# Token mixing with centred w1 columns on the split raw x, two plain queries, and DVE, POOL and loads in program order

## The chip, the cores and the metric

One core of one Trainium2 chip runs the whole program. The metric is the device time of one execution in microseconds (us). The kernel before was run three times: 1012.42, 1010.75 and 1012.12 us, so its median is 1012.12 us. The engines are PE (TensorE, matrix products), ACT (ScalarE), DVE (VectorE), POOL (GpSimd) and SP (which here only issues DMAs).

## What is computed

One input x of 2048 tokens by 448 channels goes through an attention (16 heads of 28, one shared key and value) and through a token-mixing MLP, and a gate mixes the two. Everything is float32.

```python
x = A_x
g = _sigmoid((x * gate_w).sum(-1, keepdims=True))
a = _A_ref(x, A_wq, A_wk, A_wv, A_wo)          # softmax(q k / sqrt(28)) v, then @ wo
...
h = _gelu(_layernorm(x, axis=-1) @ w1)         # 448 -> 448
...
hs = concatenate([g0, g1, g2, g3]) @ w2        # four channel groups shifted by +1, -1, +2, -2 tokens
x1 = x + hs
h2 = _gelu(_layernorm(x1, axis=-1) @ w3) @ w4  # 448 -> 1792 -> 448
...
return g * a + (1 - g) * (x1 + h2)
```

The layernorm has no weights: (x - m) / sqrt(v + eps). Because the mean over channels is linear, (x - m) @ w1 equals x @ (w1 minus the mean of each of its columns), and the division by the deviation is one factor for each token.

## The kernel before

**Arithmetic.** A float32 product is made of fp32r products of a rounded high part and a low part: `proj` (L110 to L116) issues 11 matmuls of 512 columns for a contraction over 448 channels. `proj32` (L118 to L120) is the plain float32 form, 4 matmuls. High parts are casts by ACT, low parts are subtractions by DVE (`split_w`, `split_x`, `split_a`).

**Stages.** Tokens are worked in four blocks of 512. Stage one makes, for each block b, four query tiles (`stage_q(4b)` to `stage_q(4b+3)`, which also carry keys, values and the gate; ACT copies each from PSUM and stores it to a DRAM scratch `qd`), the layernorm of x, `stage_w1(b)` (four tiles of 112 channels, each of 11 matmuls, then two Gelu passes on ACT and a subtraction on POOL) and `stage_w2(b)` (four token tiles of 12 matmuls, each added to x1 by DVE at L360). Stage two is the MLP: in each block 14 steps f, each with `w3_part` (11 matmuls) and `w4_part` for step f-2 (12 matmuls). Stage three is attention. The products of stages one and two go through two PSUM banks (`mm_tile`, tag "mm", two buffers): a product may start when the product two before it has been read out.

**The first layernorm.** `layernorm_stats` takes mean and variance on DVE and the power -0.5 on POOL; `layernorm_norm` makes the normalised rows on DVE and POOL; `layernorm_tile` transposes them on PE (L152, four transposes for each of 16 token tiles) into the "tp" banks, and `split_a` splits them again (ACT L106, DVE L107 and L108). The queries do not need it: they take the transposed x that is loaded as `xT` and split by `split_x`.

**What sets the order.** PE runs in program order throughout. In stage one a block `stage_one` puts DVE and POOL in program order too, up to the middle of the last `stage_w2`; in attention a block `attention` does so for DVE. Everywhere else, and for ACT always, a scheduler orders the instructions from its own estimates. An engine waits at the head of its queue, so what stands behind a waiting instruction waits with it. SP issues nearly all loads; `xraw` has three buffers (tag "raw", shared with `wqraw`), the raw w3 and w4 pieces have one each (`raw3`, `raw4`), so the next piece can be loaded when the last one has been split.

**Late small work.** The gate (`gg`, `gi`, L563 to L566) and the weighing of x1 by 1 - g (L671, 16 tiles on POOL) stand at the start of stage three. The first query's preparation (L535 to L544) stands in block 0 of the MLP, its maxima (`fills`) from block 1 on.

Of the kernel before, what the change touches and what calls it, by code (L numbers as in the profile page):

```python
# [9 lines left out]
F32 = mybir.dt.float32  # L10
# [30 lines left out]
def gated_mix_kernel(  # L41
# [17 lines left out]
    ctx.enter_context(tc.manual_schedule(engines={mybir.EngineType.PE}))  # L59
# [62 lines left out]
    def layernorm_stats(pool, b):  # L122
        pairs = (1, 3) if pool.name == "s1" else (3,)
        mv = pool.tile([P, 4, 2], F32, tag="mv", bufs=2, name=f"mv_{pool.name}_{b}")
        rs = pool.tile([P, 4], F32, tag="rs", bufs=2, name=f"rs_{pool.name}_{b}")
        for t in range(4):
            st = pool.tile([P, 6], F32, tag="st", bufs=4, name=f"st_{pool.name}_{b}_{t}")
            nc.vector.bn_stats(st, x1[:, 4 * b + t, :])
            nc.vector.bn_aggr(mv[:, t, :], st)
            if t in pairs:  # L130
                w = slice(t - pairs[0], t + 1)
                nc.gpsimd.tensor_tensor(rs[:, w], mv[:, w, 1], epst[:, w], ALU.add)
                nc.gpsimd.tensor_tensor(rs[:, w], rs[:, w], powt[:, w], ALU.pow)
        return mv, rs
# [3 lines left out]
    def layernorm_norm(pool, b, t, mv, rs):  # L138
        xt = x1[:, 4 * b + t, :]
        xn = pool.tile([P, 512], F32, tag="xn", bufs=3 if pool.name == "s1" else 4, name=f"xn_{pool.name}_{b}_{t}")  # L140
        nc.vector.tensor_scalar(xn[:, 0:D], xt, mv[:, t, 0:1], rs[:, t:t + 1],
                                op0=ALU.subtract, op1=ALU.mult)
        nc.gpsimd.tensor_copy(xn[:, D:512], xn[:, 384:D])
        xn_of[t] = xn
# [79 lines left out]
    with tc.tile_pool(name="s1b", bufs=1) as s1b, \  # L224
# [26 lines left out]
        for g in range(1, 4):  # L251
            nc.sync.dma_start(wqraw[:, 0:3, g * P:(g + 1) * P], wq[:, 0:3, g * P:(g + 1) * P])
        nc.sync.dma_start(wqdup[64:128], wq[64:128, 3, :])
        w1h = s1.tile([P, 4, D], F32R, name="w1h")
# [15 lines left out]
        def stage_q(u):  # L270
            b, g = divmod(u, NG)
            ps = mm_tile(f"q_{u}")
            w = slice(g * P, (g + 1) * P)
            if u < 4:
                proj32(ps, lambda c: wqraw[:, c, w], wqraw[:, 3, w], xraw[0])
            else:
                proj(ps, wqh[:, :, w], wql[:, :, w], *xact[b])
            qf = s1.tile([P, 512], F32, tag="qf", bufs=3, name=f"qf_{u}")
            nc.scalar.copy(qf, ps)
            nc.scalar.dma_start(qd[g, :, 512 * b:512 * b + 512], qf)  # L280
# [30 lines left out]
        def ln1_begin(b):  # L311
            ah = s1.tile([P, 4, 512], F32R, tag="ah", bufs=3, name=f"ah1_{b}")
            al = s1.tile([P, 3, 512], F32R, tag="al", bufs=3, name=f"al1_{b}")
            acts[b] = (ah, al, *layernorm_stats(s1, b))

        def ln1_tile(b, t):
            ah, al, mv, rs = acts[b]
            layernorm_tile(s1, tp_tile, b, t, mv, rs, ah, al)

        def ln1_norm(b, t):  # L320
            layernorm_norm(s1, b, t, *acts[b][2:4])
# [6 lines left out]
        def stage_w1(b, after):  # L328
            hh[b] = s1b.tile([P, 4, 516], F32R, tag="hh", bufs=2, name=f"hh_{b}")
            hl[b] = s1b.tile([P, 4, 516], F32R, tag="hl", bufs=2, name=f"hl_{b}")  # L330
            for m in range(4):
                ps = mm_tile(f"h_{b}_{m}")
                w = slice(m * C, (m + 1) * C)
                proj(ps[0:C, :], w1h[:, :, w], w1l[:, :, w], *acts[b][0:2])
                for job in after.get(m, ()):
                    job()
                hf = s1.tile([P, 512], F32, tag="hf", bufs=2, name=f"hf_{b}_{m}")
                nc.scalar.activation(hh[b][0:C, m, 2:514], ps[0:C, :], AF.Gelu_apprx_tanh)
# [26 lines left out]
        load_x1(0)  # L365
# [3 lines left out]
        load_x1(1)  # L369
# [6 lines left out]
        def ln_jobs(b):  # L376
            def step(t):
                ln1_tile(b, t)
                if t < 3:
                    ln1_norm(b, t + 1)  # L380
            return {m: (lambda t=m - 1: step(t),) for m in (1, 2, 3)}

        stage_one = ExitStack()
        stage_one.enter_context(tc.manual_schedule(
            engines={mybir.EngineType.PE, mybir.EngineType.DVE, mybir.EngineType.Pool}))
        stage_q(0)
        split_w(wqraw, wqh, wql, slice(0, 256), wqdup)
        stage_q(1)
        split_w(wqraw, wqh, wql, slice(256, 512), wqdup)
        stage_q(2)  # L390
        split_x(1, ((0, 2), (2, 4)))
        stage_q(3)
        ln1_begin(0)
        stage_q(4)
        ln1_norm(0, 0)
        ln1_norm(0, 1)
        ln1_norm(0, 2)
        stage_q(5)
        split_w(w1raw, w1h, w1l)
        ln1_tile(0, 0)  # L400
        ln1_norm(0, 3)
        ln1_tile(0, 1)
        stage_q(6)
        ln1_tile(0, 2)
        ln1_tile(0, 3)
        stage_q(7)
        ln1_begin(1)
        split_x(2, ((0, 2), (2, 4)))
        ln1_norm(1, 0)
        stage_w1(0, ln_jobs(1))  # L410
        stage_kv(0)
        stage_q(8)
        split_w2()
        ln1_tile(1, 3)
        stage_q(9)
        ln1_begin(2)
        ln1_norm(2, 0)
        stage_w1(1, ln_jobs(2))
        stage_kv(1)
        stage_w2(0)  # L420
        split_k(0)
        stage_q(10)
        ln1_tile(2, 3)
        stage_q(11)
        split_x(3, ((0, 2), (2, 4)))
        ln1_begin(3)
        ln1_norm(3, 0)
        stage_w1(2, ln_jobs(3))
        stage_kv(2)
        stage_w2(1)  # L430
        split_k(1)
        stage_q(12)
        ln1_tile(3, 3)
        mv0, rs0 = layernorm_stats(s1b, 0)
# [3 lines left out]
        stage_w1(3, {})  # L438
# [11 lines left out]

        def load_w34(i, pool):
            load_w3(i, pool)
            load_w4(i, pool)

        def load_w3(i, pool):
            w3h.append(pool.tile([P, 4, 2 * P], F32R, name=f"w3h_{i}"))
            w3l.append(pool.tile([P, 4, 2 * P], F32R, name=f"w3l_{i}"))
            raw = s2a.tile([P, 4, 256], F32, tag="raw3", bufs=1, name=f"w3raw_{i}")
            nc.sync.dma_start(raw, w3[:, :, i * 256:i * 256 + 256])
            split_w(raw, w3h[i], w3l[i])  # L460

        def load_w4(i, pool):
            w4h.append(pool.tile([P, 2, D], F32R, name=f"w4h_{i}"))
            w4l.append(pool.tile([P, 2, D], F32R, name=f"w4l_{i}"))
            raw = s2a.tile([P, 2, D], F32, tag="raw4", bufs=1, name=f"w4raw_{i}")
            nc.sync.dma_start(raw, w4[i * 256:i * 256 + 256, :].rearrange("(c p) n -> p c n", p=P))
            nc.scalar.copy(w4h[i], raw)
            nc.vector.tensor_tensor(w4l[i], raw, f32(w4h[i]), ALU.subtract)
# [12 lines left out]
        ln_begin(0, (mv0, rs0))  # L481
        for t in range(4):
            layernorm_norm(s2a, 0, t, *acts[0][2:4])
# [3 lines left out]
        stage_w2(NB - 1, lambda t: load_w3(0, s2a) if t == 0 else load_w4(0, s2a) if t == 1 else None)  # L487
        stage_one.close()
        for i in range(1, 3):
            load_w34(i, s2a)  # L490

    with tc.tile_pool(name="s2", bufs=1, reuse_waits="tile") as s2, \
            tc.tile_pool(name="ps2", bufs=1, space=PSUM, reuse_waits="tile") as ps2:
        fills = [lambda t=t: max_part(0, t, max_tile) for t in range(4)]
# [27 lines left out]
        for b in range(NB):  # L522
            acc = [ps2.tile([P, 512], F32, tag="acc", bufs=4, name=f"acc_{b}_{t}") for t in range(4)]
            gs = {}
            for f in range(NF):
                if f == NF - 3 and b + 1 < NB:
                    ln_begin(b + 1)
                if f == NF - 1 and b + 1 < NB:
# [3 lines left out]
                if b == 0 and f % 2 and f < 8:  # L532
                    load_w34((f + 5) // 2, s2a if f == 1 else s2)
                if b == 0 and f == 9:
# [4 lines left out]
                    q_load(0, s2.tile([P, 512], F32, tag="gf", bufs=2, name="qr_0"))  # L539
                    q_split(0, qh0, s2.tile([P, 512], F32R, tag="gl", bufs=3, name="ql_0"))  # L540
                    q_rows(0)
                if f >= 2:
                    for t in range(4):
                        w4_part(f - 2, t, gs[f - 2], acc)  # L544
                        if b > 0 and t % 2 == 0 and f < NF - 1:
# [15 lines left out]
    with tc.tile_pool(name="s3", bufs=1, reuse_waits="tile") as s3, \  # L561
            tc.tile_pool(name="ps3", bufs=1, space=PSUM, reuse_waits="tile") as ps3:
        nc.gpsimd.tensor_tensor(gg, invE, gz, ALU.pow)  # L563
        nc.vector.tensor_scalar(gg, gg, 1.0, None, op0=ALU.add)
        nc.vector.reciprocal(gg, gg)
        nc.vector.tensor_scalar(gi, gg, -1.0, 1.0, op0=ALU.mult, op1=ALU.add)  # L566

# [102 lines left out]
        for n in range(NT):  # L670
            nc.gpsimd.tensor_scalar(x1[:, n, :], x1[:, n, :], gi[:, n:n + 1], None, op0=ALU.mult)  # L671
# [31 lines left out]
        attention = ExitStack()  # L703
        attention.enter_context(tc.manual_schedule(engines={mybir.EngineType.PE, mybir.EngineType.DVE}))
# [38 lines left out]
        attention.close()  # L743
# [125 lines left out]
```

## Time and profile before

| | |
|---|---|
| median of three runs | 1012.12 us |
| the profiled execution's own time | 1012.79 us |
| its span, first to last instruction | 1011.2 us |
| mean granted TensorE clock | 0.996 |
| stage one (to the first w3 matmul) | 0 to 148.5 us |
| MLP (to the first attention matmul) | 148.5 to 432 us |
| attention and the tail | 432 to 1011.2 us |
| ACT / DVE / POOL busy over the span | 660.0 / 291.5 / 120.9 us |

The profile is one execution. A row of the timeline gives the start in us, the busy time in us, the engine, the line, the operation, and what was written from what; in brackets stands the idle time of that engine just before, with what ended it. Rows of matmuls overlap, because matmuls are pipelined: the pace of PE is read from start to start. A row of the waits gives who waited for whom: us in total, number of times, longest.

### The profile page before, as it was taken

What the parts mean: (1) busy time and instruction counts of PE and PEld (TensorE: products, weight loads), DVE (VectorE), ACT (ScalarE), POOL (GpSimd) and SP (SyncE); (2) the same over time, 40 slices, a digit from 0 to 9 for tenths busy, and PEclk for the clock granted to TensorE, in tenths of its full rate; (3) what the DMA queues carried; (4) which work ended last, traced back from release to release, by engine and by line L of the source; (5) the groups of instructions that cost most, each with busy time, mean ns of one, the idle gap of its engine ahead of it and who ended that gap; (6) DMA issues with size and microseconds to landing.
All of it is one profiled execution on the core that took longest, in us unless ns stands there. A gap on an engine that the chain in (4) does not pass through costs nothing.

```text
span 1011.2 us, 13843 instructions
## 1 busy us (share of the span) xinstructions
PE 994.1 (98%) x5336; PEld 647.7 (64%) x5336; DVE 291.5 (29%) x618; ACT 660.0 (65%) x1290; POOL 120.9 (12%) x176
## 2 busy tenths in 40 slices
PE   9999989999999999999999999999999999999996
PEld 4787878888888888854554554555455455545553
DVE  5645375342141131131222222222221222222113
ACT  4532325322232232289999989989998998999894
POOL 3333350020020020050000000000000000000000
PEclk9999999999999999999999999999999999999999
DMA  8600215200000000021011101101120110121001
GB/s 286 247 22 24 91 42 157 76 1 1 1 1 1 0 1 0 19 66 39 12 28 38 38 29 49 38 11 30 38 75 2 39 38 11 48 57 29 2 2 40
DMA packets 34085, 43.68 MB, mean 43 GB/s; under 512 B 9004, under 2 KB 22108, under 8 KB 34012
## 3 DMA queue, kind: packets, MB, share of 16 engines
q1 hardware_dynamic: 31228, 38.20, 13.1%
q10 hardware_dynamic: 2784, 4.52, 1.2%
q8 instruction: 44, 0.72, 0.3%
q14 instruction: 29, 0.24, 0.1%
HBM read 23.15 MB, written 7.86 MB: 31 GB/s over the span
## 4 chain that ended last, share of the span: by engine, by line
PE 92%; DVE 3%; POOL 1%; DMA 1%; ACT 1%; issue 0%; SPq 0%; POOLq 0%; ACTq 0%
PE bank L718 26%; PE pv L694 23%; PE acc L518 4%; PE acc L520 4%; PE acc L519 4%; PE g L112 4%; PE g L114 4%; PE g L113 4%; PE q L120 2%; PE bank L652 2%; PE bank L187 1%; PE bank L656 1%; PE bank L654 1%; PE g L115 1%; PE g L116 1%; PE h L113 1%
## 5 line engine op out<-in xcount | busy, mean ns | idle before, releaser
L720 ACT ACTIVATE p<-bank 128x512 f32<-128x512 f32 x1024 | 515.1, 629 | 47.9 <-PE bank L718 45.4
L718 PE MATMUL bank<-qs,kS 98*128 98x512 f32 x1024 | 316.3, 411 | 0.5 <-DVE x L556 0.5
L718 PEld LDWEIGHTS bank<-qs,kS 98*128 98x128 f32 x1024 | 183.2, 189 | 147.6 <-issue 106.5
L694 PE MATMUL pv<-p,vext 128*32 128x512 f32 x2048 | 246.5, 598 | 0.0
L508 ACT ACTIVATE gh<-g 128x512 fp32r<-128x512 f32 x56 | 33.5, 599 | 156.5 <-PE g L116 156.4
L694 PEld LDWEIGHTS pv<-p,vext 128*32 128x32 f32 x2048 | 54.8, 109 | 114.6 <-issue 108.9
L188 DVE TENSOR_REDUCE mr<-bank 128x4 f32<-128x512 f32 x60 | 41.6, 693 | 168.3 <-PE bank L187 168.3
L510 DVE TENSOR_TENSOR gl<-gf,gh 128x512 fp32r<-128x512 f32 x56 | 38.6, 691 | 158.6 <-ACT gf L509 154.2
L661 DVE SCALAR_TENSOR_TENSOR ot<-bank,gg,ot 128x448 f32<-128x448 f32 x48 | 32.8, 684 | 174.7 <-PE bank L656 89.0
L518 PE MATMUL acc<-w4h,gh 128*128 128x448 f32 x224 | 82.1, 367 | 0.0
L520 PE MATMUL acc<-w4h,gl 128*128 128x448 f32 x224 | 81.5, 364 | 0.0
L519 PE MATMUL acc<-w4l,gh 128*128 128x448 f32 x224 | 81.3, 363 | 0.0
L639 POOL CAST onh<-on 128x512 fp32r<-128x512 f32 x15 | 9.2, 612 | 501.4 <-DVE on L636 501.4
L112 PE MATMUL g<-ah,w3h 128*128 128x512 f32 x168 | 66.0, 393 | 0.9 <-ACT gf L509 0.9
L114 PE MATMUL g<-ah,w3l 128*128 128x512 f32 x168 | 65.6, 391 | 0.0
L113 PE MATMUL g<-al,w3h 128*128 128x512 f32 x168 | 65.6, 391 | 0.0
L519 PEld LDWEIGHTS acc<-w4l,gh 128*128 128x128 f32 x224 | 42.1, 188 | 4.3
L518 PEld LDWEIGHTS acc<-w4h,gh 128*128 128x128 f32 x224 | 42.1, 188 | 4.2
L520 PEld LDWEIGHTS acc<-w4h,gl 128*128 128x128 f32 x224 | 42.1, 188 | 3.2
L671 POOL TENSOR_SCALAR x<-x,gi 128x448 f32<-128x448 f32 x16 | 23.1, 1458 | 130.0 <-DVE x L556 130.0
L114 PEld LDWEIGHTS g<-ah,w3l 128*128 128x128 f32 x168 | 31.5, 188 | 6.8
L112 PEld LDWEIGHTS g<-ah,w3h 128*128 128x128 f32 x168 | 31.6, 188 | 6.7 <-ACT gf L509 1.3
(186 smaller groups left out, 1022.3 us busy)
## 6 DMA issues: line engine op xcount, KB each, us to landing
qs<-qh SPq DMA_DIRECT2D x32, 224.0 KB
qd<-qf ACTq DMA_DIRECT2D x16, 256.0 KB
x<-in_x_dram SPq DMA_DIRECT2D x4, 896.0 KB
w3raw<-in_w_dram SPq DMA_DIRECT2D x7, 512.0 KB
qr<-qd SPq DMA_DIRECT2D x16, 224.0 KB
qs<-ql SPq DMA_DIRECT2D x16, 224.0 KB
out_dram<-ot SPq DMA_DIRECT2D x16, 224.0 KB
w4raw<-in_w_dram SPq DMA_DIRECT2D x7, 448.0 KB
```

The costliest lines, as they stand in the source:

```text
L112: nc.tensor.matmul(ps, wh[:, c, :], ah[:, c, :], start=(c == 0), stop=False)
L113: nc.tensor.matmul(ps, wh[:, c, :], al[:, c, :], start=False, stop=False)
L114: nc.tensor.matmul(ps, wl[:, c, :], ah[:, c, :], start=False, stop=False)
L188: nc.vector.reduce_max(mx_of[u][:, :, t], ps, axis=AX.X)
L508: nc.scalar.activation(gh, ps, AF.Gelu_apprx_tanh)
L510: nc.vector.tensor_sub(gl, gf, f32(gh))
L518: nc.tensor.matmul(ps, gh[:, tok], w4h[i][:, k, :], start=(f == 0), stop=False)
L519: nc.tensor.matmul(ps, gh[:, tok], w4l[i][:, k, :], start=False, stop=False)
L520: nc.tensor.matmul(ps, gl[:, tok], w4h[i][:, k, :], start=False, stop=(f == NF - 1))
L694: nc.tensor.matmul(pv[32 * j:32 * j + 32, :], vext[:, kt, :], ps[j], start=(kt == 0), stop=(kt == NT - 1), tile_position=(0, 32 * j))
L718: nc.tensor.matmul(ps, kS[0:98, kt * P:(kt + 1) * P], q_of[u][0:98, j, :], start=True, stop=True)
L720: nc.scalar.activation(p, ps, AF.Exp, scale=SCALE)
```

## The change

1. **No normalised x for w1.** `stage_w1` now multiplies the split raw x (`xact[b]`, the same operand as the queries) by w1 whose columns have been centred. POOL sums w1 over its row chunks (`sum_w1`), one plain float32 matmul with a matrix of ones sums over partitions, and DVE subtracts the mean from w1 (`centre_w1`) before w1 is split. The 1/deviation of each token is stored to DRAM, loaded back broadcast over 112 partitions (`ln1`), and DVE multiplies it onto each product; the two Gelu passes then read that from SBUF. The 64 transposes, the normalised rows and their split are gone.
2. **Two plain queries instead of four**; x of block 0 is now split as well.
3. **Order.** DVE, POOL and SP run in program order for the whole kernel, and the program's text is rearranged: loads stand where they are to be issued, `stage_w1(0)` and `stage_w1(1)` follow each other, each w3/w4 piece's load is separated from its split, the normalisation for the next MLP block has its own place at f = 12, the first query's preparation and maxima move one block later, the gate moves to MLP block 1, and twelve of the sixteen weighings of x1 to MLP block 3.

```diff
-    ctx.enter_context(tc.manual_schedule(engines={mybir.EngineType.PE}))
+    ctx.enter_context(tc.manual_schedule(
+        engines={mybir.EngineType.PE, mybir.EngineType.DVE, mybir.EngineType.Pool, mybir.EngineType.SP}))
...
-            if u < 4:
+            if u < 2:
                 proj32(ps, lambda c: wqraw[:, c, w], wqraw[:, 3, w], xraw[0])
...
+        def ln1(b):
+            _, rs = layernorm_stats(s1, b)
+            rd = dram.tile([1, 512], F32, tag="rsd", bufs=2, name=f"rsd_{b}")
+            nc.sync.dma_start(rd.rearrange("o (t p) -> p (o t)", p=P), rs)
+            rb_of[b] = s1.tile([P, 512], F32, tag="rsb", bufs=2, name=f"rsb_{b}")
+            nc.sync.dma_start(rb_of[b][0:C], rd.broadcast_to([C, 512]))
...
+        def sum_w1():
+            nc.gpsimd.tensor_tensor(wsum, w1raw[:, 0, :], w1raw[:, 1, :], ALU.add)
+            nc.gpsimd.tensor_tensor(wsum, wsum, w1raw[:, 2, :], ALU.add)
+            nc.gpsimd.tensor_tensor(wsum[0:64], wsum[0:64], w1raw[0:64, 3, :], ALU.add)
+
+        def centre_w1():
+            ps = misc_tile("wsum_ps")[:, 0:D]
+            nc.tensor.matmul(ps, ones, wsum, start=True, stop=True)
+            for c in range(4):
+                nc.vector.scalar_tensor_tensor(w1raw[:, c, :], ps, -1.0 / D, w1raw[:, c, :],
+                                               op0=ALU.mult, op1=ALU.add)
...
-                proj(ps[0:C, :], w1h[:, :, w], w1l[:, :, w], *acts[b][0:2])
...
-                hf = s1.tile([P, 512], F32, tag="hf", bufs=2, name=f"hf_{b}_{m}")
-                nc.scalar.activation(hh[b][0:C, m, 2:514], ps[0:C, :], AF.Gelu_apprx_tanh)
-                nc.scalar.activation(hf[0:C, :], ps[0:C, :], AF.Gelu_apprx_tanh)
+                proj(ps[0:C, :], w1h[:, :, w], w1l[:, :, w], *xact[b])
+                hf = s1.tile([P, 512], F32, tag="hf", bufs=3, name=f"hf_{b}_{m}")
+                nc.vector.tensor_mul(hf[0:C, :], ps[0:C, :], rb_of[b][0:C, :])
+                nc.scalar.activation(hh[b][0:C, m, 2:514], hf[0:C, :], AF.Gelu_apprx_tanh)
+                nc.scalar.activation(hf[0:C, :], hf[0:C, :], AF.Gelu_apprx_tanh)
...
+        load_x1(0)
+        load_x1(1)
+        stage_q(0)
+        split_x(0, ((0, 2), (2, 4)))
+        split_w(wqraw, wqh, wql, slice(256, 512), wqdup)
+        stage_q(1)
+        stage_q(2)
+        split_w(wqraw, wqh, wql, slice(0, 256), wqdup)
+        split_x(1, ((0, 2), (2, 4)))
+        stage_q(3)
+        sum_w1()
+        ln1(0)
+        load_x(2)
...
+        stage_q(4)
+        centre_w1()
+        stage_q(5)
+        stage_q(6)
+        split_w(w1raw, w1h, w1l)
+        ln1(1)
+        load_x(3)
+        load_x1(3)
         stage_q(7)
...
+        stage_w1(0)
+        split_w2()
         split_x(2, ((0, 2), (2, 4)))
...
+        stage_w1(1)
+        stage_kv(1)
+        ln1(2)
         stage_q(8)
...
+        def weights(t):
+            if t % 2 == 0:
+                split_w3(t // 2)
+            else:
+                split_w4(t // 2)
+                load_w34(t // 2 + 1, s2a)
+
+        stage_w2(NB - 1, weights)
...
+                if b == 1 and f == 0:
+                    nc.gpsimd.tensor_tensor(gg, invE, gz, ALU.pow)
...
+                if b == NB - 1 and f == 4:
+                    weigh_x1(0, 4 * b)
```

More of the change, by code (lines that the diff above doesn't have):

```diff
@@ L129, in layernorm_stats @@
             nc.vector.bn_aggr(mv[:, t, :], st)
[L130 to L133, printed above, removed]
+        nc.gpsimd.tensor_tensor(rs, mv[:, :, 1], epst, ALU.add)
+        nc.gpsimd.tensor_tensor(rs, rs, powt, ALU.pow)
         return mv, rs
@@ L309, in stage_v @@
             nc.vector.tensor_copy(gz.rearrange("p (b t) -> p t b", t=4), vp[:, :, :, DH])
[L311 to L321, printed above, removed]
+        rb_of = {}
+        def ln1(b):
[4 more added lines that the diff above has]
+            nc.sync.dma_start(rb_of[b][0:C], rd.broadcast_to([C, 512]))
+        ones = s1.tile([P, P], F32, name="ones")
+        nc.gpsimd.memset(ones, 1.0)
+        wsum = s1.tile([P, 512], F32, tag="hf", bufs=3, name="wsum")[:, 0:D]
+        def sum_w1():
[8 more added lines that the diff above has]
+                                               op0=ALU.mult, op1=ALU.add)
         def split_w2():
@@ L372, in gated_mix_kernel @@
         load_x1(2)
+        stage_q(4)
[4 more added lines that the diff above has]
+        ln1(1)
         load_x(3)
         load_x1(3)
[L376 to L405, printed above, removed]
         stage_q(7)
-        ln1_begin(1)
+        stage_w1(0)
+        split_w2()
         split_x(2, ((0, 2), (2, 4)))
-        ln1_norm(1, 0)
-        stage_w1(0, ln_jobs(1))
         stage_kv(0)
+        stage_w1(1)
+        stage_kv(1)
+        ln1(2)
         stage_q(8)
-        split_w2()
-        ln1_tile(1, 3)
         stage_q(9)
[L416 to L421, printed above, removed]
         stage_q(10)
-        ln1_tile(2, 3)
         stage_q(11)
         split_x(3, ((0, 2), (2, 4)))
-        ln1_begin(3)
-        ln1_norm(3, 0)
-        stage_w1(2, ln_jobs(3))
+        split_k(0)
         stage_kv(2)
+        ln1(3)
+        stage_w2(0)
+        stage_w1(2)
+        mv0, rs0 = layernorm_stats(s1b, 0)
+        split_k(1)
         stage_w2(1)
-        split_k(1)
         stage_q(12)
-        ln1_tile(3, 3)
-        mv0, rs0 = layernorm_stats(s1b, 0)
         stage_q(13)
@@ L527, in gated_mix_kernel @@
                     ln_begin(b + 1)
+                if f == NF - 2 and b + 1 < NB:
+                    for t in range(4):
+                        layernorm_norm(s2a, b + 1, t, *acts[b + 1][2:4])
                 if f == NF - 1 and b + 1 < NB:
@@ L668, in gated_mix_kernel @@
         nc.gpsimd.tensor_tensor(wol, woraw, f32(woh), ALU.subtract)
-        for n in range(NT):
-            nc.gpsimd.tensor_scalar(x1[:, n, :], x1[:, n, :], gi[:, n:n + 1], None, op0=ALU.mult)
+        weigh_x1(NT - 4, NT)
         jobs = []
```

68 lines of the change are left out of this document (31 added, 37 removed).

## The prediction

> **What bounds the kernel now.** I read the page first: busy shares, then the chain of waits.
>
> ```profile
> span 1011.2 us, 13843 instructions
> PE 994.1 (98%) x5336; PEld 647.7 (64%) x5336; DVE 291.5 (29%) x618; ACT 660.0 (65%) x1290; POOL 120.9 (12%) x176
> ...
> PE 92%; DVE 3%; POOL 1%; DMA 1%; ACT 1%; issue 0%; SPq 0%; POOLq 0%; ACTq 0%
> ```
>
> PE is busy for 98% of the span and makes 92% of the chain that ends last. An edit is therefore worth the PE work that it takes away or adds and the PE waits that it ends or makes; the rest is cover. So next the waits of PE, and the busy times by stretches of 25 us (this row: length, then PE, PEld, DVE, ACT, POOL busy, granted clock, DMA share, GB/s):
>
> ```profile
> PE hs L356 <- DVE x L360: 3.2, 1, 3.2
> ...
> PE g L112 <- ACT gf L509: 0.9, 1, 0.9
> ...
> PE q L120 <- DMA xkv<-in_xT_dram: 0.7, 1, 0.7
> ```
> ```profile
> 125.00:150.00 25.00, 21.82 (x106) 19.18 (x105) 17.80 (x45) 6.13 (x11) 14.99 (x28) 0.93 0.18 56
> ```
>
> PE is busy for only 21.82 of these 25 us, at a granted clock of 0.93. The timelines of PE, POOL and DVE tell how:
>
> ```profile
> 135.87 0.37 PE L358 MATMUL hs<-w2h,hl 112*128 112x448 f32 x1
> 139.41 0.47 PE L356 MATMUL hs<-w2h,hh 112*128 112x448 f32 x1 [3.18 <-DVE x L360]
> ...
> 140.46 0.57 PE L357 MATMUL hs<-w2l,hh 112*128 112x448 f32 x1
> 140.83 0.57 PE L358 MATMUL hs<-w2h,hl 112*128 112x448 f32 x1
> ```
> ```profile
> 133.57 2.91 POOL L563 TENSOR_TENSOR gg<-invE,gz 128x16 f32<-128x16 f32 x1
> ...
> 136.73 1.01 POOL L133 TENSOR_TENSOR rs_s2a<-rs_s2a,powt 128x4 f32<-128x4 f32 x1
> ```
> ```profile
> 137.77 0.94 DVE L141 TENSOR_SCALAR xn_s2a<-x,mv_s2a,rs_s2a 128x448 f32<-128x448 f32 x2 [5.74 <-POOL rs_s2a L133]
> ```
>
> The scheduler put the gate's power (2.91 us) and the second MLP block's layernorm here. POOL does the gate first, DVE stands 5.74 us at the head of its queue for POOL, and the add to x1 that frees PE's bank is behind it. After 3.18 us idle the matmuls run 0.37 us apart instead of 0.20.
>
> **What is removed.** (a) That stall. The gate moves to MLP block 1, the statistics of block 1 to f = 11 of block 0, and in program order nothing stands between the adds but splits of w3 and w4. Gain: 3.3 us from start to start beyond one step, and nine matmuls at 0.37 against 0.20 us, 1.5 us: 4.8 us.
>
> (b) The wait at MLP step 3: between these starts lie 1.29 us where 0.20 is a step, 1.1 us.
>
> ```profile
> 158.18 0.37 PE L520 MATMUL acc<-w4h,gl 128*128 128x448 f32 x1
> 159.47 0.50 PE L112 MATMUL g<-ah,w3h 128*128 128x512 f32 x1 [0.92 <-ACT gf L509]
> ```
>
> The Gelu it waited for stood behind a cast of w4 in ACT's queue; in the changed program it stands ahead of it. What is late next is the w3 piece of step 4, loaded after the split of the piece before, some 2 us earlier in the stage than now. I take the whole 1.1 us.
>
> (c) The transposes for w1, one group of four for each of 16 token tiles:
>
> ```profile
> L152 PE MATMUL tp_s<-ident,xn_s 128*128 128x128 f32 x64 | 9.7, 275 | 1.3 <-DVE xn_s L141 0.9 <-POOL xn_s L143 0.4
> ```
> ```profile
> 42.45 0.60 PE L152 MATMUL tp_s<-ident,xn_s 128*128 128x128 f32 x4
> 42.81 0.47 PE L112 MATMUL h<-ah,w1h 128*112 128x512 f32 x1
> 43.12 0.39 PE L113 MATMUL h<-al,w1h 128*112 128x512 f32 x1
> ```
>
> From start to start a group takes 0.36 us, and the first matmul behind it 0.31 instead of 0.23: 0.44 us, 16 times, 7.0 us. Its waits, 1.3 us, go too.
>
> (d) Two queries become split ones. ACT copies each query out as it ends, so these copies give the pace, plain and then split:
>
> ```profile
> 18.44 0.59 ACT L279 COPY qf<-q 128x512 f32<-128x512 f32 x1 [1.90 <-PE q L120]
> ...
> 21.88 0.59 ACT L279 COPY qf<-q 128x512 f32<-128x512 f32 x1 [0.67 <-PE q L120]
> ...
> 24.39 0.59 ACT L279 COPY qf<-q 128x512 f32<-128x512 f32 x1 [1.34 <-PE q L116]
> ...
> 26.89 0.59 ACT L279 COPY qf<-q 128x512 f32<-128x512 f32 x1 [1.91 <-PE q L116]
> ```
>
> 3.44 against 2.50 us: 1.9 us for two. (e) x's first chunks are now issued ahead of all wq pieces of SP; the 0.7 us wait bounds the gain, and I take 0.4.
>
> Together 4.8 + 1.1 + 7.0 + 1.3 + 1.9 + 0.4 = 16.5 us.
>
> **What is added on PE's path.** (f) The sum of w1's columns is one plain matmul of 448 columns: 3.44 / 4 x 448 / 512 = 0.75 us.
>
> (g) DVE between the first two w1 blocks. In program order the split of w2 and of x block 2 stand behind the fourth multiply of block 0 and ahead of the first multiply of block 1, and that multiply frees the bank that PE wants two products later. The pace of a w1 product is read at two Gelus; a multiply of 512 columns out of PSUM is not in the trace, its nearest row is the maximum over 512 columns of PSUM:
>
> ```profile
> 54.44 0.60 ACT L338 ACTIVATE hh<-h 112x512 fp32r<-112x512 f32 x1 [2.15 <-DMA qd<-qf]
> ...
> 56.97 0.60 ACT L338 ACTIVATE hh<-h 112x512 fp32r<-112x512 f32 x1 [1.45 <-PE h L116]
> ```
> ```profile
> L188 DVE TENSOR_REDUCE mr<-bank 128x4 f32<-128x512 f32 x60 | 41.6, 693 | 168.3 <-PE bank L187 168.3
> ```
> ```profile
> 22.96 1.73 DVE L101 TENSOR_TENSOR w1l<-w1raw,w1h 128x448 fp32r<-128x448 f32 x3
> ...
> 36.26 1.79 DVE L266 TENSOR_TENSOR alk<-xkv,ahk 128x1024 fp32r<-128x1024 f32 x2
> 38.06 0.69 DVE L267 TENSOR_TENSOR ahk<-xkv,ahk 64x512 fp32r<-64x512 f32 x1
> ...
> 48.02 3.17 DVE L326 TENSOR_TENSOR w2l<-w2raw,w2h 112x448 fp32r<-112x448 f32 x4
> ```
>
> From the end of block 0's last product DVE needs 0.69 (multiply), 2.3 to 3.17 (four parts of w2: at w1's rate, or as they ran beside POOL), 1.79 + 0.69 (x) and 0.69 (multiply): 6.2 to 7.0 us. PE is there after two products, 2 x 2.53 = 5.06 us. A wait of 1.1 to 2.0 us; I take 1.6.
>
> (h) The deviation's way through DRAM delays x block 2. On SP the store and the broadcast load of block 0's deviation now stand ahead of the load of x block 2, and in ACT's queue the first cast of that block stands ahead of the copy of query 7, whose bank PE needs for the second w1 product. PE: query 4 started at 21.27, less (d) and (e) 19.0; 4 queries of 2.5, (f) and one product of 2.53 give 32.3 us. The chain against it starts with the statistics, which in the profile run from 18.02:
>
> ```profile
> 18.02 0.63 DVE L128 BATCH_NORM_STATS2 st_s<-x 128x6 f32<-128x448 f32 x1
> ...
> 20.86 0.18 DVE L129 BATCH_NORM_AGGREGATE mv_s<-st_s 128x2 f32<-128x6 f32 x1
> ```
> ```profile
> 964.29 0.62 SPq L615 DMA_DIRECT2D rt<-o  x1
> ```
> ```profile
> 966.21 0.18 DVE L609 SCALAR_TENSOR_TENSOR good<-rt,good 128x16 f32<-128x16 f32 x1 [4.64 <-DMA rt<-o]
> ```
> ```profile
> 144.65 0.61 SPq L459 DMA_DIRECT2D w3raw<-in_w_dram  x1
> ```
> ```profile
> 148.59 0.83 ACT L97 CAST w3h<-w3raw 128x768 fp32r<-128x768 f32 x1 [14.16 <-DMA w3raw<-in_w_dram]
> ```
> ```profile
> 28.50 2.00 ACT L264 CAST ahk<-xkv 128x1024 fp32r<-128x1024 f32 x2
> ```
>
> One more split of x precedes the statistics, but DVE idled before; I take 18.5 to 21.5, then 1.2 on POOL: 22.7. The store moves 512 single floats. The nearest row, 128 pieces of 16 floats, landed 1.92 us after its issue; four times that, 7.7, is the other bound. I take 3, nearer the row, as both move 8 KB or less. Then 0.6 to issue the broadcast. The 1 MB load lies between the 512 KB one (3.94 us to its cast) and twice that, 7.9; I take 6, since the broadcast and the copies of queries share the engines. With the cast (1.0) and the copy (0.6) the bank is free at 33.9: PE waits 1.6 us. Low bounds: 30.7, no wait. High bounds: 40.5, 8.2 us.
>
> (i) On the last w1 block the multiply puts POOL's work 0.69 us later, less a 0.3 us memset moved away, and the first normalised tile of the MLP just met PE before: 0.4 us (0 to 0.9). (j) Queue order elsewhere: 0.5 (0 to 2).
>
> Added: 0.75 + 1.6 + 1.6 + 0.4 + 0.5 = 4.85 us.
>
> **What costs nothing, and its cover.** The other 14 multiplies (0.69) fit in 2.53 us a product, and free the bank sooner than two Gelus did. The centring on DVE (four of 0.69) and the split of w1 behind it have three queries, 7.5 us, and need some 6; without that cover each us late is a us of PE. In the MLP a step is 4.97 us and DVE idles for most of it, which covers maxima, gate and normalisation:
>
> ```profile
> 421.01 0.69 DVE L510 TENSOR_TENSOR gl<-gf,gh 128x512 fp32r<-128x512 f32 x1 [4.27 <-ACT gf L509]
> ```
>
> The weighing, 12 of 1.46 us on POOL, falls where POOL is idle. Attention keeps PE's, ACT's and DVE's order.
>
> **The sum.** 16.5 - 4.85 = 11.65 us. The profiled execution took 1012.79 us, 0.7 above the median of 1012.12; the difference is taken from the median: 1000.5 us.
>
> The Trainium skill, TensorE: Matmul & The Clock Gate, Part 1: The HAM clock gate, says that the clock is halved after an idle window of about 3.4 us. The 3.18 us wait, with a granted clock of 0.93 behind it, roughly agrees. By that rule waits of 1.6 us leave the clock alone and the sum stands; if waits of that length trip it as the long one did, each costs 1.5 us more, and with two of them the sum would be 1003.5 us.
>
> **Rivals.** *The covers hold:* (h), (i) and (j) cost nothing and (g) 1.1: 1012.12 - 16.5 + 1.85 = 997.5 us. For it: every bound's low end; against: the order in ACT's queue.
>
> *x block 2 is late by more:* store 5 and load 7.5 us make (h) 5.1, and a wait that long halves the clock as at 139.41, 1.5: 1005.5. For it: DMA is shared just then.
>
> *The change does not end the stall (a):* DVE now waits in program order for the second w3 piece ahead of the last add; if that reaches PE, 4.8 us stay: 1005.3. Against: no matmul of stage one needs that last add.
>
> *Slower, through the store:* single floats to DRAM are in no row. From a store of about 13 us on (0.4 us for each of the 32 floats that fall to one of 16 engines), the wait (h) with its halved clock eats the whole gain; at 16 us 1015 us. Against: twice the upper bound. The Trainium skill, DMA: Bandwidth & Descriptors, Rules for kernel authors, says that a last dimension without contiguous elements becomes one descriptor for each element, and Specifications, that pieces below 512 B are read, modified and written; it gives no time for them.
>
> **How the numbers follow.** Forecast 1000.5 us, 58%, with its own range 997 to 1004; covers hold 12%; x late 15%; stall stays 7%; slower 8%. The range, 996.5 to 1006.5, takes in the first four but for their tails. 0.2% (2 us) is about what a measurement tells from no change. Faster by more: all of the first two, 13 of 15 and 6 of 7: 89%. Same: 3%. Slower: 8%.
>
> **What would show it.** Right: no transposes before the MLP; query copies 2.5 us apart from the third on; PE without a wait of 3 us at the end of stage one; a wait of PE for DVE of 1 to 2 us at the third product of w1 block 1, and one for ACT near 32 us at the second of block 0; the first w3 matmul near 138 us and attention 578 us long. Wrong: PE waits in the MLP, a clock under 1.0 in stage one, or a store whose broadcast lands after 33 us.

## The result and the profile after

| | before | after |
|---|---|---|
| median, us | 1011.58 (1010.22 to 1014.25, 15 runs) | 1014.84 (1013.10 to 1016.28, 15 runs) |
| ratio to before | | 1.0032, 95% interval 1.0023 to 1.0040 |
| span of the profiled execution, us | 1011.2 | 1012.5 |
| first w3 matmul of the MLP, us | 148.5 | 150.5 |
| first attention matmul, us | 431.96 | 434.18 |

The change made the kernel slower, by 0.2 to 0.4%; 1000.5 us was forecast. The loss lies ahead of the MLP. The page after, then PE's waits (total, times, longest):

```profile
span 1012.5 us, 13677 instructions
...
PE 985.5 (97%) x5280; PEld 642.3 (63%) x5280; DVE 289.0 (29%) x593; ACT 656.5 (65%) x1277; POOL 121.7 (12%) x156
```
```profile
PE h L113 <- ACT qf L277: 12.4, 1, 12.4
PE h L113 <- DVE hf L347: 1.1, 1, 1.1
...
PE m L185 <- DVE mr L186: 0.9, 2, 0.5
...
PE tp_s2a L150 <- POOL xn_s2a L141: 0.7, 1, 0.7
```

PE is busy 8.6 us less than before (994.1 then), though 5.1 us of matmuls ran at half clock: the removed work is gone. The 3.2 us wait of before is gone as well. In its place stands one wait of 12.4 us, at the place of step (h). The stretches of 25 us (columns as in the prediction) and two short ones around the wait:

```profile
25.00:50.00 25.00, 12.62 (x47) 9.49 (x46) 5.97 (x14) 8.16 (x14) 1.22 (x2) 0.74 0.98 149
...
125.00:150.00 25.00, 24.35 (x127) 21.57 (x126) 13.80 (x28) 7.77 (x13) 9.35 (x21) 1.00 0.24 70
```
```profile
36.50:45.40 8.90, 0.00 (x0) 0.00 (x0) 0.69 (x1) 1.54 (x3) 0.00 (x0) 0.51 0.93 235
45.40:50.50 5.10, 5.06 (x12) 3.70 (x13) 0.00 (x0) 3.93 (x7) 0.39 (x1) 0.51 1.17 198
```

The end of the stage, 0.93 in clock before, now runs at 1.00. Between 25 and 50 us PE works half the time. The clock is halved while PE stands, which costs nothing, and for 5.1 us after: 12 matmuls take 5.14 us from start to start where 2.76 is their pace, so about 2.4 us are lost. The wait follows back along three timelines, SP's issues, then ACT, then PE:

```profile
24.09 0.37 SPq L314 DMA_DIRECT2D rsd<-rs_s  x1
34.31 0.34 SPq L316 DMA_DIRECT2D rsb<-rsd  x1
34.88 0.55 SPq L233 DMA_DIRECT2D xkv<-in_xT_dram  x1
...
37.45 0.74 SPq L314 DMA_DIRECT2D rsd<-rs_s  x1
56.32 0.34 SPq L316 DMA_DIRECT2D rsb<-rsd  x1
...
76.31 0.38 SPq L314 DMA_DIRECT2D rsd<-rs_s  x1
85.36 0.30 SPq L316 DMA_DIRECT2D rsb<-rsd  x1
```
```profile
43.85 1.04 ACT L262 CAST ahk<-xkv 128x1024 fp32r<-128x1024 f32 x1 [15.19 <-DMA xkv<-in_xT_dram]
44.81 0.58 ACT L277 COPY qf<-q 128x512 f32<-128x512 f32 x1
```
```profile
32.66 0.40 PE L117 MATMUL h<-ahk,w1l 128*112 128x512 f32 x1
45.44 0.77 PE L113 MATMUL h<-ahk,w1h 128*112 128x512 f32 x1 [12.38 <-ACT qf L277]
```

The broadcast can go out only when the store has landed, and SP issues in order. So the distance between the two issues is the store's time: 10.2 us, 18.9 for the second, which shares the engines with 2.7 MB of loads, and 9.0 for the third. The load of x block 2 goes out 10.8 us after the store; its cast stands ahead of the copy of query 7 in ACT's queue, and that copy frees PE's bank.

What moves meanwhile is seen in the DMA view of 24 to 36 us (40 slices of 0.3 us: busy tenths, then GB/s):

```profile
DMA  9525201000069900090090000090030009969978
GB/s 355 178 61 4 2 0 0 0 0 0 0 232 362 137 0 0 0 27 0 0 14 0 0 0 0 0 20 0 0 7 0 0 0 75 96 68 198 143 184 246
```

Most of the store's time moves nothing at all. The 2.7 MB of loads are not issued yet, because SP stands behind the store; but ACT has handed over two stores of queries (at 26.6 and 28.7 us). Of these 0.2 MB move from 27.3 to 28.2 us, and then next to nothing until 33.9.

### The profile page after: what moved, and what is told of

Same layout as the page of the kernel before. It is cut to its first block, busy times and chain, and to the rows that moved or that the text cites. A ratio compares the mean times of both kernels' runs of the same rounds, so it can differ in the third digit from the quotient of the medians.

```text
span 1012.5 us, 13677 instructions
## 1 busy us (share of the span) xinstructions
PE 985.5 (97%) x5280; PEld 642.3 (63%) x5280; DVE 289.0 (29%) x593; ACT 656.5 (65%) x1277; POOL 121.7 (12%) x156
## 4 chain that ended last, share of the span: by engine, by line
PE 91%; DMA 5%; DVE 2%; ACT 1%; issue 0%; POOL 0%; SPq 0%; ACTq 0%; POOLq 0%
PE bank L722 26%; PE pv L700 23%; PE acc L516 4%; PE acc L518 4%; PE acc L517 4%; PE g L113 4%; PE g L115 4%; PE g L114 4%; DMA rsd<-rs_s 3%; PE bank L659 2%; PE bank L185 1%; PE g L116 1%; PE g L117 1%; PE bank L663 1%; PE bank L661 1%; PE hs L367 1%
## 5 line engine op out<-in xcount | busy, mean ns | idle before, releaser
L114 PEld LDWEIGHTS g<-al,w3h 128*128 128x128 f32 x168 | 31.6, 188 | 5.5
```

The source lines that it names most:

```text
L114: nc.tensor.matmul(ps, wh[:, c, :], al[:, c, :], start=False, stop=False)
```

## Experiments

Each edit is to the changed kernel, unless another is named; `...` in a diff marks lines left out. Waits and spans are those of the profiled execution.

**Size of the pieces.**

```diff
-            nc.sync.dma_start(rd.rearrange("o (t p) -> p (o t)", p=P), rs)
+            k = 2 if b == 2 else 4
+            nc.sync.dma_start(rd.rearrange("o (h p k) -> p (o h) k", p=P, k=k),
+                              rs.rearrange("p (h k) -> p h k", k=k))
```

> The store of the deviations goes out in 128 pieces of 16 bytes (for x block 2 in 256 pieces of 8 bytes) in place of 512 single floats; queues, order and every engine's program stay. The deviations reach other tokens than their own by this. Theory (the number of pieces): store plus its completion fell from 10.2 us to about 2.5 us for the first block, 18.9 to under 6 for the second, about 4.5 for the third (half the pieces of the 9.0) and 2.3 for the fourth (a quarter of the 8.2). The broadcast and the load of x block 2 go out some 7.7 us earlier, ScalarE's cast of that block too, and the 12.4 us wait of TensorE shrinks to about 5 (12.4 - 7.7), with the clock still halved for one or two steps of 3.41 us; span about 1004 (1002 to 1006), ratio to before about 0.993. Rival (a trip through DRAM at this place, whatever its pieces): store still 8 us or more, span 1012. Rival (ScalarE's order alone): the wait only moves, 10 us or more of it stay, span over 1009.

Measured: 1007.76 us, ratio 0.9962 (0.9949 to 0.9976), span 1005.4. SP's queue of this kernel:

```profile
23.88 0.34 SPq L315 DMA_DIRECT2D rsd<-rs_s  x1
26.88 0.34 SPq L318 DMA_DIRECT2D rsb<-rsd  x1
...
32.51 0.35 SPq L315 DMA_DIRECT2D rsd<-rs_s  x1
44.12 0.33 SPq L318 DMA_DIRECT2D rsb<-rsd  x1
...
66.39 0.38 SPq L315 DMA_DIRECT2D rsd<-rs_s  x1
71.00 0.30 SPq L318 DMA_DIRECT2D rsb<-rsd  x1
```

The store takes 3.0 us, the third, of twice as many pieces, 4.6. Only the shape of the pieces differs, and 7 us come back. The second still takes 11.6 us where under 6 was expected: the loads stand ahead of it, and only 7.3 of its 18.9 went with the pieces. PE still waits 5.8 us, since a store of 3.0 us, the broadcast's issue and a load of 9.6 us lie between the deviations and ACT's cast.

**The order on ACT.** `stage_q(7)` to `split_x(3)` are put under a schedule that takes ACT in program order too.

```diff
+        with tc.manual_schedule(engines={mybir.EngineType.PE, mybir.EngineType.DVE, mybir.EngineType.Pool,
+                                         mybir.EngineType.SP, mybir.EngineType.Activation}):
...
```

> ScalarE takes program order too from query 7 to the split of x block 3, so that the copy of query 7 stands ahead of the cast of x block 2; the store stays as it is. Theory (the store with two ways to reach TensorE): query 7 is copied at about 31 us and the second hidden block of the first w1 step runs until 35.5, but the third must wait for the first multiply, which the broadcast releases at 39.9: a wait of about 5 us (40.6 - 35.5) on VectorE's multiply in place of the 12.4 on ScalarE, clock still halved once or twice; span about 1004.5 (1003 to 1007). Rival (ScalarE's order alone): no wait over 1 us is left there, span 997 to 999. Rival (the trip through DRAM is not what holds TensorE): the wait stays at 12 us.

Measured: 1028.39 us, ratio 1.0171 (1.0157 to 1.0185), span 1026.0. PE's waits, then ACT and its DMA issues:

```profile
PE h L113 <- DVE hf L347: 12.7, 2, 6.8
PE hs L366 <- DVE x L370: 9.6, 1, 9.6
```
```profile
77.41 0.59 ACT L277 COPY qf<-q 128x512 f32<-128x512 f32 x1 [1.91 <-PE q L117]
84.25 0.33 ACTq L278 DMA_DIRECT2D qd<-qf  x1
84.62 1.99 ACT L262 CAST ahk<-xkv 128x1024 fp32r<-128x1024 f32 x2 [6.62 <-DMA qd<-qf]
```

At its place the theory holds: the 12.4 us become 5.9. The forecast of the total misses by 21.5 us, because the other stores then come into the open: the second leaves 6.8 us, and during the third, 72.5 to 83.6 us, ACT stands 6.6 us at the issue of a query's store, behind which in program order is the cast that DVE and then PE wait for. So the scheduler's order on ACT alone was not the cause. In the changed kernel the first wait covers the second store: PE comes to the multiply of block 1 so late that the deviations are there. The third wait is of this edit's own making, since there ACT's cast of x block 3 stands behind the copy of query 11 only by this order; the experiment with both edits below shows it.

**The loads first.**

```diff
-        ln1(0)
         load_x(2)
...
         load_x1(2)
+        ln1(0)
```

> The loads of x block 2, w2 and the third block of x rows are issued ahead of the store and broadcast of block 0 (the order part of the change undone at this place); ScalarE's scheduler then also puts w2's casts ahead of query 7's copy. Theory: the loads go out at about 10 us and the cast of x block 2 waits for nothing, but the single-float store now runs among them as the second store did (18.9 us), so that the multiply comes at 24 + 10 to 19 + 5.5, 40 to 49 us, and TensorE waits 4 to 12 us for VectorE: span 1003 to 1013. Rival (only the load behind the store counts): wait gone, span 997 to 999.

Measured: 1014.10 us, ratio 1.0023 (1.0013 to 1.0034), span 1013.1. The store takes 15.3 us now, among the loads, and PE waits 4.6 us for the multiply. Before that the copy of query 7 waits on ACT, for a cause that was not in the forecast:

```profile
34.34 0.59 ACT L277 COPY qf<-q 128x512 f32<-128x512 f32 x1 [4.12 <-DMA qd<-qf]
```

Its buffer is still being stored from: the store of query 4, handed over at 23.30, just ahead of the floats at 23.67, is done only 11 us later. That is a third way to PE, by ACT's own stores, and PE waits 2.4 us by it. Moving the loads only trades ways.

**Without the trip.** The deviations are spread by PE, which reads a column as 112 equal ones:

```diff
...
-            rd = dram.tile([1, 512], F32, tag="rsd", bufs=2, name=f"rsd_{b}")
-            nc.sync.dma_start(rd.rearrange("o (t p) -> p (o t)", p=P), rs)
-            rb_of[b] = s1.tile([P, 512], F32, tag="rsb", bufs=2, name=f"rsb_{b}")
-            nc.sync.dma_start(rb_of[b][0:C], rd.broadcast_to([C, 512]))
+            rs_of[b] = rs
+
+        def spread(b):
+            ps = tp_tile(f"rsp_{b}")
+            for t in range(4):
+                nc.tensor.transpose(ps[0:C, t * P:(t + 1) * P], rs_of[b][:, t:t + 1].to_broadcast([P, C]), ident)
+            rb_of[b] = s1.tile([P, 512], F32, tag="rsb", bufs=2, name=f"rsb_{b}")
+            nc.vector.tensor_copy(rb_of[b][0:C], ps[0:C])
...
+            spread(b)
```

> No store and no broadcast: four transposes of the deviation column, read 112 times, write the spread deviations into PSUM ahead of each w1 step, and VectorE copies them to SBUF once a block. Added on TensorE: 16 transposes at 0.11 us, 1.8 us, perhaps twice that for their weight loads. Theory (the store and what stood behind it cost 14.9 us: 12.4 of wait and 13.65 us of half clock of which about 5 us were work): span 1012.5 - 14.9 - 1.1 (second block's wait) + 1.8 = 998.3 (996.5 to 1000.5), ratio to before 0.986 to 0.989; granted clock 0.996 or better; no wait over 1 us on TensorE in the first 100 us. Rival (the rest of the change, centring, order or clock, costs part of the time): span over 1003 with no long wait.

Measured: 1001.95 us, ratio 0.9911 (0.9898 to 0.9925), span 999.7, clock 0.998. The four transposes of a block take 0.35 us from the first to the matmul behind them, which itself takes 0.31 us where 0.23 is a step: 0.43 us, 1.7 in all. The one long wait left, 2.3 us where none over 1 was expected, is step (g): DVE makes the splits in one piece ahead of the multiply, and with them the copy that this edit adds.

```profile
40.86 0.69 DVE L352 TENSOR_TENSOR hf<-h,rsb 112x512 f32<-112x512 f32 x1 [1.93 <-PE h L117]
41.46 2.22 DVE L341 TENSOR_TENSOR w2l<-w2raw,w2h 112x448 fp32r<-112x448 f32 x4
43.60 1.82 DVE L264 TENSOR_TENSOR alk<-xkv,ahk 128x1024 fp32r<-128x1024 f32 x2
45.44 1.49 DVE L265 TENSOR_TENSOR ahk<-xkv,ahk 64x512 fp32r<-64x512 f32 x1
46.96 0.69 DVE L320 COPY rsb<-rsp 112x512 f32<-112x512 f32 x1
47.79 1.29 DVE L352 TENSOR_TENSOR hf<-h,rsb 112x512 f32<-112x512 f32 x2
```

**The splits between the multiplies**, in the kernel without the trip:

```diff
...
-        stage_w1(0)
-        split_w2()
-        split_x(2, ((0, 2), (2, 4)))
+        stage_w1(0, [lambda m=m: split_w2(m) for m in range(4)])
         stage_kv(0)
-        stage_w1(1)
+        stage_w1(1, split_x_jobs(2))
```

> The kernel without store and broadcast (deviations spread by TensorE), and in it the splits of w2 and of x block 2 no longer stand in one piece between the w1 steps of blocks 0 and 1 on VectorE, but one small part behind each multiply. Theory: the 2.3 us that TensorE waits there for the first multiply of block 1 are VectorE's 2.22 + 1.82 + 0.69 us of splits; spread over eight hidden blocks of 2.5 us each they hide. Span 999.7 - 2.3 = 997.4 (996.5 to 998.5), ratio to before about 0.987 to 0.989, no wait over 0.5 us on TensorE before 130 us. Rival (the wait comes from elsewhere, as from the copy of the spread deviations on VectorE or from ScalarE): it stays, span 999 to 1000.

Measured: 999.78 us, ratio 0.9875 (0.9860 to 0.9890), span 997.9; no wait of 0.5 us is left on PE between 9 and 100 us, and the 0.7 us of step (i) stays further on. This is the fastest of the kernels here, faster than the kernel before and the changed one.

**Both single edits**, pieces and order on ACT together:

> Both single edits together: store in 128 pieces of 16 bytes (256 of 8 bytes for x block 2; the deviations reach other tokens by it) and ScalarE in program order from query 7 to the split of x block 3. Theory (two ways from the store to TensorE, and each store counts): the first block's wait is gone (below 1 us), where either edit alone left 5.8 and 5.9; the second store, which runs among loads (11.6 us with wide pieces), leaves 2 to 5 us on the first multiply of block 1; the third, at 4.6 us, 0 to 3 us where ScalarE now waits in order behind query copies; span 1003 (1000 to 1006). Rival (one cause alone): no better than the better of the two alone, span 1005 or more.

Measured: 1009.53 us, ratio 0.9970 (0.9955 to 0.9984), span 1006.0. The first block's wait is gone, and the other two are 3.6 and 3.4 us where 2 to 5 and 0 to 3 were expected. In the total the rival is right, for another reason: it is no better than the wide pieces alone (1005.4), because what the first block gives is taken back later. The 3.6 us belong to the second store, which took 9.8 us among the loads. The 3.4 us do not belong to the third:

```profile
64.90 0.59 ACT L277 COPY qf<-q 128x512 f32<-128x512 f32 x1 [1.91 <-PE q L117]
65.93 2.00 ACT L262 CAST ahk<-xkv 128x1024 fp32r<-128x1024 f32 x2 [0.44 <-ACT qf L277]
```

That store had landed at 64.2 us. ACT waits for PE's query 11, copies it and only then casts x block 3, as the edit orders; DVE waits 8.4 us for the cast, and the add that PE needs stands behind it.

**Four plain queries**, in the kernel without the trip:

```diff
-            if u < 2:
+            if u < 4:
```

> The kernel with the deviations spread by TensorE, but four plain queries as before the change. Theory (term d of the prediction): two queries of 4 plain matmuls in place of 11 split ones cost 1.9 us on TensorE and nothing stands ahead of them, span 999.7 + 1.9 = 1001.6 (1001 to 1002.5). Rival (the time before the split weights are ready is idle time that plain queries fill): span within 0.5 us of 999.7.

Measured: 1006.86 us, ratio 0.9944 (0.9930 to 0.9957), span 1003.2, 3.5 more and not 1.9. The stretch behind the 2.3 us wait, here and in the kernel with two plain queries:

```profile
50.00:55.00 5.00, 4.25 (x13) 3.13 (x14) 1.48 (x3) 2.42 (x4) 2.18 (x2) 0.71 0.00 0
```
```profile
50.00:55.00 5.00, 5.00 (x23) 3.87 (x22) 1.69 (x3) 2.57 (x5) 3.24 (x3) 1.00 0.00 0
```

After the same wait, 2.26 and 2.27 us, the clock was halved here and not there. The spreading of block 1's deviations, ahead of that wait, starts at

```profile
42.80 0.60 PE L318 MATMUL rsp<-ident,rs_s 128*112 128x128 f32 x4
```
```profile
40.59 0.60 PE L318 MATMUL rsp<-ident,rs_s 128*112 128x128 f32 x4
```

So 2.2 us are lost before, near the 1.9 of term (d), and they hold some small waits besides. Behind the wait, at the first matmul of query 8 (57.50 and 53.73 us), it is 3.8: the halved clock took 1.6. This split is that of the profiled execution alone: another one of this kernel, with a clock of 0.998 over its span, took 1003.1 us, and the medians differ by 4.9 us. That two more plain queries cost time is shown; how much stays open.

**The price of the pieces by itself**, in the MLP, with no load due:

```diff
...
+                if b == 2 and f == 0:
+                    for k, (dst, src) in enumerate(trials):
+                        nc.sync.dma_start(dst, src)
+                        nc.sync.dma_start(back[0:1, k:k + 1], spots[k][0:1, 0:1])
```

> The kernel with the deviations spread by TensorE, and in the MLP, where SP has nothing due, eight stores of other data to spots of their own in DRAM, each followed by a read of it, whose issue shows when the store has landed. Store to read, in us, for: 512 single floats side by side; 512 single floats 512 bytes apart; 512 pieces of 64 bytes; 512 pieces of 512 bytes; 256 of 8 bytes; 128 of 16 bytes; 4 of 512 bytes; 512 single floats again. Theory (a price for each piece under 512 bytes, some 16 ns, one after another): 9, 9, 9, under 3, 4.6, 2.5, 2, 9. Rival (pieces that fall into one short stretch of DRAM wait for each other): 9, under 3, under 3, under 3, 4.6, 2.5, 2, 9. Rival (a price only beside loads or by the place in the kernel): all under 3. The span stays at 999.7, plus at most 1.

Measured, one run: span 1001.6, 1.9 more than without them where at most 1 was expected, with a halved clock behind the 2.3 us wait again (0.997 over the span). SP's queue holds the answers as distances from each store (L576) to its read (L577):

```profile
237.17 0.54 SPq L576 DMA_DIRECT2D spot<-ident  x1
246.19 0.26 SPq L577 DMA_DIRECT2D back<-spot  x1
246.50 0.36 SPq L576 DMA_DIRECT2D spot<-kS  x1
249.57 0.24 SPq L577 DMA_DIRECT2D back<-spot  x1
249.85 0.36 SPq L576 DMA_DIRECT2D spot<-kS  x1
251.62 0.24 SPq L577 DMA_DIRECT2D back<-spot  x1
...
254.47 0.36 SPq L576 DMA_DIRECT2D spot<-ident  x1
258.64 0.24 SPq L577 DMA_DIRECT2D back<-spot  x1
```

| store | us to its read |
|---|---|
| 512 floats side by side | 9.0, again 8.9 |
| 512 floats, 512 bytes apart | 3.1 |
| 512 pieces of 64 bytes | 1.8 |
| 512 pieces of 512 bytes | 2.3 |
| 256 of 8 bytes side by side | 4.2 |
| 128 of 16 bytes side by side | 1.4 |
| 4 of 512 bytes | 2.1 |

My theory, a price for each small piece, falls; the rival of the short stretch comes nearest (3.1 us where it said under 3, and 1.4 where both said 2.5). The same 512 floats cost a third when each has its own stretch of DRAM, and as many pieces of 64 bytes cost 1.8 us. What costs is many pieces that fall into one short stretch.

**The trip, with nobody waiting for it**, beside the deviations spread by PE:

```diff
...
+            nc.sync.dma_start(rd.rearrange("o (t p) -> p (o t)", p=P), rs)
+            spare = s1.tile([P, 512], F32, tag="spare", bufs=1, name=f"spare_{b}")
+            nc.sync.dma_start(spare[0:C], rd.broadcast_to([C, 512]))
```

> The multiplies take the deviations that TensorE spreads, and the changed kernel's store and broadcast stay as well, in the same places of SP's queue, but into a tile that nothing reads; ScalarE has the cast of x block 2 ahead of the copy of query 7 as in the changed kernel. Theory (the trip holds TensorE mainly by what stands behind it on SP): x block 2 is issued near 35 us as before, ScalarE's cast at 43.9, TensorE waits 12 us (12.4 less 0.4 for the transposes) on the copy of query 7 though no multiply waits, clock halved; span 1011 to 1013. Rival (the multiply that waits for the broadcast is the cause): no wait over 2.5 us, span 999 to 1001.

Measured: 1016.96 us, ratio 1.0052 (1.0035 to 1.0068), span 1013.8, no better than the changed kernel. PE, which no deviation holds here:

```profile
43.90 0.77 PE L113 MATMUL h<-ahk,w1h 128*112 128x512 f32 x1 [11.04 <-ACT qf L277]
```

So the wait comes by what stands behind the store on SP, not by the multiply that needs its result; that one alone would hold PE for 5.9 us, as the order on ACT showed. The span is 0.8 us above the expected range, and PE waits 1.5 and 1.6 us for later multiplies.

**The removed transposes put back**, in the fastest kernel, 64 with a result that nothing reads:

```diff
+                extra = tp_tile(f"extra_{b}_{m}")
+                for t in range(4):
+                    nc.tensor.transpose(extra[:, t * P:(t + 1) * P], x1[:, 4 * b + m, t * 64:t * 64 + P], ident)
```

> The best kernel so far (deviations spread by TensorE, splits between the multiplies), and ahead of each of its 16 w1 hidden blocks four transposes of 128 by 128 whose result nothing reads: the PE work that term c of the prediction said the change takes away. Theory: 16 x 0.44 = 7.0 us more, span 997.9 + 7.0 = 1004.9 (1004.3 to 1006). Rival (transposes of this kind run in the shadow of the matmuls' pipeline): under 4 us, span below 1002.

Measured: 1006.16 us, ratio 0.9941 (0.9924 to 0.9958), span 1004.8: 6.9 us more, against 7.0.

## Why the prediction was wrong

**The step that failed is (h)**, by its size; its mechanism, place and chain were as described. The wait was taken as 1.6 us, at most 8.2, and was 12.4. Its terms:

| term of (h) | taken, us | measured, us |
|---|---|---|
| store issued | 22.7 | 24.1 |
| store until the broadcast's issue | 3 (1.92 to 7.7) | 10.2 |
| broadcast's issue | 0.6 | 0.57 |
| load of x block 2 to its cast | 6 (3.94 to 7.9) | 9.0 |
| PE at the bank | 32.3 | 33.1 |

The late parts add up to 1.4 + 7.2 + 3.0 - 0.8 = 10.8 us, and 1.6 + 10.8 is the 12.4. Two choices were wrong. The store was put near the row of 128 pieces of 16 floats because it moves few bytes; bytes do not price it, nor does the number of pieces, so that 7.7 was no upper bound. Pieces of 64 bytes, as in that row, cost 1.8 us even when there are 512. That row was no store to DRAM either: `o` and `rt` are both tiles on the chip. And the load was taken in the middle between one of half its size and twice that, though it goes out right behind a broadcast and with two more loads on its heels. What made it 9.0 us stays open: with the same neighbours it took 9.6 with the wide pieces and 6.6 with the idle trip.

**The slower rival** came true in kind, but its point was set too high: 10.2 us of store sufficed where about 13 were asked, since the store went out 1.4 us later and the load took 3 us longer than it reckoned. It had 8%.

**(a)** right: the 3.2 us wait is gone and the clock there is 1.00. **(b)** the wait at MLP step 3 is gone, yet the time from the first w3 matmul to attention is 283.7 us, as before (283.5): 0.9 us are given back where the maxima of the first queries wait for one bank (the wait on line 185), which no step had by name. **(c)** right: 6.9 us for the transposes. **(d)** is near the 2.2 us lost ahead of the wait with four plain queries, in one execution; its size stays open. **(e)** is lost in how much the waits at the start differ between kernels (0.7 us before, 0.5 after, 1.8 in the fastest); it stays open. **(f)** right: from the start of the sum (22.09) to the second matmul behind it (23.08) lie 0.99 us where 0.23 is a step, 0.76 against 0.75. **(g)** 1.1 us, the low end; without the trip 2.3 us, of which 0.7 is the copy that this edit adds, so 1.6, as taken, but in part by luck: the last row of the split of x (L265) took 1.49 us there where 0.69 was counted, and the split of w2 2.22, less than either rate. **(i)** 0.7 us, in its bounds. **(j)** named no place; the 0.9 us on line 185 is a wait of its kind.

The sum without (h) was 16.5 - 3.25 = 13.25 us. Less 1.7 for the transposes that spread the deviations, 11.55; the kernel without the trip gained 1011.2 - 999.7 = 11.5. In stage one the terms that fall there give 15.4 - 4.45 = 10.95 (removed: all but (b); added: (f), (g), (i) and the 1.7), and 11.0 were gained (148.5 to 137.5). Beyond it the agreement is luck: the MLP took 283.7 us as in the changed kernel, so the 1.1 of (b) did not come, and attention with the tail took 578.5 us against 579.2, which no term had. From that kernel to the changed one lie 12.8 us: the waits, 12.4 + 1.1 - 2.3, 2.4 of half clock, less the 1.7, make 11.9, and 0.7 more are a later start of the first w1 product (30.37 against 30.00) and a wait of 0.3 us at a query.

**The clock.** The prediction let waits of 1.6 us leave the clock alone. Which waits do so is not told by their length here. Clock 1.00 followed waits of 1.1 us (changed kernel), 1.5 and 1.6 (idle trip), 2.27 (without the trip) and 3.6 (both single edits); a halved clock followed waits of 1.8 and 2.4 (loads first), 2.26 (twice), 3.2 (before) and 3.4 (both single edits). The loads-first kernel behind its wait of 1.8 us, then the one with both edits, its wait of 3.6 us (it ends at 49.5) and the stretch behind it:

```profile
64.92 0.50 PE L113 MATMUL q<-ahk,wqh 128*128 128x512 f32 x1 [1.78 <-DVE hf L347]
...
66.58 0.63 PE L113 MATMUL q<-ahk,wqh 128*128 128x512 f32 x1
```
```profile
PE h L113 <- DVE hf L349: 3.6, 1, 3.6
```
```profile
50.00:55.00 5.00, 5.00 (x24) 3.77 (x23) 0.77 (x3) 3.58 (x6) 2.59 (x3) 1.00 0.59 185
```

In the first the matmuls lie 0.43 us apart from 66.58 on, where 0.23 is a step; in the second the clock is 1.00. The Trainium skill, TensorE: Matmul & The Clock Gate, Part 1: The HAM clock gate, describes an activity window of about 3.4 us that runs freely. That where a wait falls in such a window decides would fit these waits; no run here moves a wait alone to show it.

Of the signs that the prediction named, the end of the stall, the wait of 1 to 2 us for DVE and attention's 578 us (578.3) came; the first w3 matmul, called for near 138 us, came at 150.5, and at 137.5 in the kernel without the trip. All three signs of being wrong came too: a wait in the MLP (0.9 us), a clock under 1.0 in stage one (0.74 from 25 to 50 us), and a broadcast after 33 us (issued at 34.3).

Open: how long the stretch of DRAM is within which small pieces hold each other, and why other queues stand still meanwhile.

## What to carry to other kernels

Price a store to DRAM by how its pieces lie, and not by its bytes: single floats from 128 partitions, side by side, were the worst of the cases tried (9.0 us). Wider pieces (16 bytes from each partition 1.4 us, four rows of 512 bytes 2.1) or a spread by TensorE avoid it. A transfer that is itself short on the critical path must be costed with all that its queue holds behind it, here a 1 MB load. Where one long wait is shortened, look for the same operation further on: here the second store was covered by the first.

## What was not expected of the hardware

- 512 single floats side by side take 9.0 us to land, 512 bytes apart 3.1, and pieces of 64 bytes 1.8. The Trainium skill, DMA: Bandwidth & Descriptors, Specifications, names 512 bytes as the size below which a piece is read, modified and written; by time the runs show no step between 64 and 512 bytes (512 pieces of 64 bytes 1.8 us, of 512 bytes 2.3).
- While such a store was under way the DMA engines moved next to nothing for most of 8 us, and stores from ACT's queue stood too; ACT waited 4.1 us (loads first) and 6.6 us (order on ACT) for them.
- The length of a wait of PE did not tell whether the clock was halved behind it: 1.8 us was followed by a halved clock, 3.6 us was not.
